# Linear attention and a feed-forward layer on one Trainium2 core: plain fp32 projections for the first two batches, and a place of its own for each loaded pair

## The chip, the cores and the metric

The kernel runs on one core of a Trainium2 chip. The metric is the device time in microseconds; the number shown is the median of three runs. Beside it stands one execution taken with the profiler, in which every instruction has a start and a length.

The engines are TensorE (matmul; the profile calls it PE, and its weight load PEld), VectorE (DVE), ScalarE (ACT), GpSimd (POOL) and SyncE (SP, which here issues all DMA transfers).

## The reference

Eight batches, eight heads, 576 tokens, head size 64; 128 features. `q`, `k` and `w_phi` are scaled so that the exponentials spread widely.

```python
def phi(x):
    proj = np.einsum('bhsd,df->bhsf', x, w_phi)
    proj = proj - np.max(np.abs(proj), axis=-1, keepdims=True)
    return np.concatenate([np.exp(proj), np.exp(-proj)], axis=-1)
q_p, k_p = phi(q), phi(k)
kv = np.einsum('bhsf,bhsd->bhfd', k_p, v)
z = np.sum(k_p, axis=2)
num = np.einsum('bhsf,bhfd->bhsd', q_p, kv)
den = np.einsum('bhsf,bhf->bhs', q_p, z)[..., None] + 1e-06
attn = (num / den).astype(np.float32)
# x: attn as 4608 tokens of 512
h = x @ w_in                       # 512 -> 2048, the weights are float64
out = np.maximum(0.01 * h, h) @ w_out   # 2048 -> 512
```

## The kernel before

**Pairs of heads.** Two heads share the 128 partitions (64 features each), so there are 32 pairs: `i = 4 * batch + pair`. Pairs 0 to 3 are batch 0 and go through `first_k_phase` and `first_q_phase`; pairs 4 to 7 are batch 1 and go through `k_phase` (its branch `nat`, for `i < NK`) and `token_q_phase`; all later pairs go through the other branch of `k_phase` and through `q_phase`, which the change leaves as they are.

**A projection.** For 128 tokens, `proj` multiplies the tokens (the stationary operand) with `bd`, a block-diagonal 128 x 256 copy of `w_phi` for both heads. It does this in three matmuls of the type float32r (`F32R`, the profile's `fp32r`): tokens and weights are both split into a high part (the value cast to float32r) and a low part (the remainder), and the products high x high (L304), high x low (L305) and low x high (L306) are summed. The splits are made once for each loaded tile: a cast for the high part (L196, L351, L452 by ScalarE, L522 by VectorE) and a subtraction for the low part (L197, L352, L453, L524). `copy_` and `tt_` (L64, L71) choose the engine: for the key's low part GpSimd and VectorE take turns, for the query's it is GpSimd. Other matmuls of these two batches, the product of exponentials and v (L212 in the branch `nat`, L484) and the numerators (L333, L567), have plain fp32 operands.

**After a projection** VectorE takes the largest absolute value of each token (L240, L317, L472, L537) and subtracts it (L243, L318, L474, L539), ScalarE makes both exponentials, TensorE the product.

**The weights.** `load_weights` brings `w_in` and `w_out` in 32 chunks as 64-bit floats through two staging places (the transfers of L154) and turns each into a high and a low float32r part: on ScalarE L159, L164 and the cast of `copy_("h")`; on VectorE L160, L161, L162, L165 and the subtraction of `tt_("l")`.

**The feed-forward part** works on 18 blocks of 256 tokens: `layer1` (L619 to L627) and `layer2` (L638 to L640), each with 16 steps over the hidden layer.

**Order.** Nothing in the text fixes the order of the instructions on an engine. A planner takes them by priority (a smaller number first) as a simulation says that their operands and places are free: first the loads of the start (`2 * PF`), then batch 0's keys and its first 256 queries (`PF`), its other queries (`PU`), the later attention (`PA`), the weights (`PW`), the feed-forward part (0). Within an engine and within SP's queue that order is then fixed, and the chip waits where an operand isn't there.

**Places.** `st(...)` takes a place from a small ring by its tag; most tags, `rk`, `rv`, `rq`, `ks` and `qs` among them, have one. A new tile with that tag waits until everything that reads the old one has run. In batch 0, pairs 0 and 2 use the places `rk` and `rv`, and pairs 1 and 3 share a place in `f2`; the loads of pairs 2 and 3 follow when the pair before them has been split or used. `fr1`, `f2`, `f3` and `fr4` are four places of 8 KB a partition which later hold the last group of weights.

## Time and profile before

| | us |
|---|---|
| median of 3 runs | 1211.63 (1211.42 to 1212.69) |
| the profiled execution | 1209.61 |
| its span, first to last instruction | 1207.8 |
| granted TensorE clock, mean | 0.992 |

| engine | busy, us | share of the span | instructions |
|---|---|---|---|
| PE | 1160.7 | 96% | 7654 |
| PEld | 1041.8 | 86% | 7654 |
| DVE | 785.4 | 65% | 1541 |
| ACT | 850.7 | 70% | 2144 |
| POOL | 437.9 | 36% | 436 |

How to read it: "busy" counts from start to end of each instruction. Matmuls overlap, so PE can look busy without doing all it could; the distance from one matmul's start to the next says more. `L304` is line 304 of the kernel; a line in a helper, such as L67 or L72, gathers all that use the helper, and the tile names (`ks<-rk`) tell them apart. In a group, `xN | busy, mean` gives count, total in us and the mean in ns, then the idle time before the group and what ended it. In a line of the timeline the columns are start, length, engine, line, operation, tiles.

### The profile page before, as it was taken

The numbers are of one execution on the slowest core, as the hardware profiler recorded it, in microseconds if no ns is written. First come the engines' busy times: TensorE is split into PE (matmuls) and PEld (weight loads), VectorE is DVE, ScalarE is ACT, GpSimd is POOL, SyncE is SP. The second block draws the span as 40 slices with busy tenths as digits, with TensorE's granted clock in tenths as the row PEclk, the third lists the DMA queues.
The fourth block names the chain that finished last, engine by engine and source line by source line (L and its number), as shares of the span: only waits on it lengthen the run. The fifth ranks groups of instructions, "written<-read, shape, count | busy, mean of one in ns | idle before, by whom it ended". The sixth has DMA issues, their size and how long they took to land.

```text
span 1207.8 us, 21459 instructions
## 1 busy us (share of the span) xinstructions
PE 1160.7 (96%) x7654; PEld 1041.8 (86%) x7654; DVE 785.4 (65%) x1541; ACT 850.7 (70%) x2144; POOL 437.9 (36%) x436
## 2 busy tenths in 40 slices
PE   6889899999998999999999999999999999999998
PEld 5578688999897988989899999998999998988987
DVE  7999864577787677677787787736777776211111
ACT  6898765778777787878888888846787877433222
POOL 3121121344544454544545454513454544210000
PEclk9999999999998999999999999999999999999999
DMA  6545421011111011111111111100111100000000
GB/s 195 149 126 150 130 80 35 22 49 31 49 32 49 21 27 43 31 49 31 49 32 49 32 40 31 49 22 28 32 49 32 49 1 19 1 18 9 10 18 18
DMA packets 62778, 57.01 MB, mean 47 GB/s; under 512 B 45136, under 2 KB 46288, under 8 KB 62672
## 3 DMA queue, kind: packets, MB, share of 16 engines
q1 hardware_dynamic: 62672, 55.65, 16.4%
q8 instruction: 60, 0.98, 0.4%
q14 instruction: 46, 0.38, 0.1%
HBM read 46.20 MB, written 9.44 MB: 46 GB/s over the span
## 4 chain that ended last, share of the span: by engine, by line
PE 76%; DVE 11%; ACT 7%; issue 3%; DMA 2%; POOL 0%; DVEq 0%; ACTq 0%
PE h L619 10%; PE h L620 10%; PE h L622 10%; PE acc L638 9%; PE acc L640 9%; PE acc L639 9%; PE c L212 6%; PE a L232 2%; PE a L422 2%; PE a L419 2%; PE a L420 2%; PE a L333 1%; DVE ql L165 1%; PE a L379 1%; PE a L380 1%
## 5 line engine op out<-in xcount | busy, mean ns | idle before, releaser
L619 PE MATMUL h<-xh,w0h 128*128 128x256 f32 x1152 | 292.3, 284 | 6.8 <-DVE gl L627 4.5
L620 PE MATMUL h<-xh,w0l 128*128 128x256 f32 x1152 | 289.7, 282 | 0.0
L627 DVE TENSOR_TENSOR gl<-h,gh 128x256 fp32r<-128x256 f32 x288 | 118.5, 416 | 237.4 <-ACT gh L67 210.9
L638 PE MATMUL acc<-w1h,gh 128*128 128x512 f32 x576 | 230.3, 400 | 6.8 <-ACT gh L67 6.1
L619 PEld LDWEIGHTS h<-xh,w0h 128*128 128x128 f32 x1152 | 217.9, 189 | 17.3 <-DVE gl L627 7.7
L639 PE MATMUL acc<-w1l,gh 128*128 128x512 f32 x576 | 228.4, 397 | 0.0
L620 PEld LDWEIGHTS h<-xh,w0l 128*128 128x128 f32 x1152 | 217.8, 189 | 6.0
L625 ACT ACTIVATE h<-h 128x256 f32<-128x256 f32 x288 | 105.3, 368 | 157.2 <-PE h L622 155.3
L640 PE MATMUL acc<-w1h,gl 128*128 128x512 f32 x576 | 204.3, 397 | 0.0
L622 PE MATMUL h<-xl,w0h 128*128 128x256 f32 x1152 | 200.1, 282 | 0.1
L72 POOL TENSOR_TENSOR ql<-eq,qh 128x576 fp32r<-128x576 f32 x96 | 146.1, 1538 | 73.0 <-ACT qh L67 47.8
L622 PEld LDWEIGHTS h<-xl,w0h 128*128 128x128 f32 x1152 | 164.3, 189 | 0.9 <-POOL xl L72 0.3
L72 POOL TENSOR_TENSOR kpl<-ek,kph 128x512 fp32r<-128x512 f32 x72 | 95.4, 1325 | 146.4 <-ACT kph L67 67.5
L638 PEld LDWEIGHTS acc<-w1h,gh 128*128 128x128 f32 x576 | 108.8, 189 | 28.4 <-ACT gh L67 9.8
L639 PEld LDWEIGHTS acc<-w1l,gh 128*128 128x128 f32 x576 | 109.0, 189 | 18.6 <-issue 0.4
L67 ACT CAST gh<-h 128x256 fp32r<-128x256 f32 x288 | 105.2, 373 | 25.6 <-PE acc L639 21.3
L72 POOL TENSOR_TENSOR xl<-ring,xh 128x256 fp32r<-128x256 f32 (+3 forms) x96 | 61.2, 669 | 155.0 <-PE h L622 135.3
L72 POOL TENSOR_TENSOR ring<-ring,mb 128x576 f32<-128x576 f32 (+2 forms) x45 | 49.8, 1108 | 175.0 <-DVE mb L342 45.5
L640 PEld LDWEIGHTS acc<-w1h,gl 128*128 128x128 f32 x576 | 99.5, 189 | 8.5 <-issue 0.4
L202 DVE TENSOR_TENSOR ks<-rk,ks 64x576 fp32r<-64x576 f32 x48 | 53.7, 1118 | 36.5 <-ACT ks L67 35.3
L250 ACT ACTIVATE ek<-pmk 128x256 f32<-128x256 f32 (+1 forms) x128 | 53.4, 417 | 24.3 <-POOL kpl L72 10.3
L212 PE MATMUL c<-kph,vh 128*66 128x256 f32 x240 | 62.3, 282 | 4.0 <-DVE kvl L295 2.2
(225 smaller groups left out, 2366.2 us busy)
## 6 DMA issues: line engine op xcount, KB each, us to landing
out_dram<-o SPq DMA_DIRECT2D x35, 256.0 KB, 2.1
rk<-in_k_dram SPq DMA_DIRECT2D x30, 288.0 KB, 2.8
ring<-in_w_in_dram SPq DMA_DIRECT2D x16, 512.0 KB, 3.6
qh<-in_w_out_dram SPq DMA_DIRECT2D x16, 512.0 KB, 3.7
rq<-in_q_dram SPq DMA_DIRECT2D x28, 288.0 KB, 3.0
rv<-in_v_dram SPq DMA_DIRECT2D x30, 256.0 KB, 3.4
rv<-in_vt_dram SPq DMA_DIRECT2D x60, 32.0 KB, 3.0
f<-in_k_dram SPq DMA_DIRECT2D x2, 288.0 KB, 4.0
```

The costliest lines, as they stand in the source:

```text
L67: nc.scalar.copy(o, i)
L72: (nc.vector if pick(key) == "v" else nc.gpsimd).tensor_tensor(o, a, b, op=op)
L202: nc.vector.tensor_tensor(ks[n, j], rk[o], ks[o, j].bitcast(F32), op=ALU.subtract)
L212: nc.tensor.matmul(kvp[0 : lt.shape[1], 256 * j : 256 * j + 256], lhsT=lt, rhs=rt, start=first and j == 0, stop=last, skip_group_check=True)
L619: nc.tensor.matmul(ph, lhsT=weight(0, "h", ft)[:, d * P : d * P + P], rhs=xh[:, d], start=d == 0, stop=False)
L620: nc.tensor.matmul(ph, lhsT=weight(0, "l", ft)[:, d * P : d * P + P], rhs=xh[:, d], start=False, stop=False)
L622: nc.tensor.matmul(ph, lhsT=weight(0, "h", ft)[:, d * P : d * P + P], rhs=xl[:, d], start=False, stop=d == NP - 1)
L625: nc.scalar.activation(ph, ph, AF.Prelu, alpha=0.01)
L627: nc.vector.tensor_tensor(gl, ph, gh.bitcast(F32), op=ALU.subtract)
L638: nc.tensor.matmul(a, lhsT=gh[:, ts], rhs=weight(1, "h", ft), start=ft == 0, stop=False)
L639: nc.tensor.matmul(a, lhsT=gh[:, ts], rhs=weight(1, "l", ft), start=False, stop=False)
L640: nc.tensor.matmul(a, lhsT=gl[:, ts], rhs=weight(1, "h", ft), start=False, stop=ft == NFT - 1)
```

## The change

`bd` becomes one plain fp32 tile, and `proj` one plain matmul that reads the loaded tile itself. The high and low parts of keys and queries of batches 0 and 1 go, with their casts and subtractions, on all of `first_k_phase`, `first_q_phase`, `k_phase` (branch `nat`) and `token_q_phase`. `rk` and `rq` are thereby read until the last projection of a phase. The four pairs of batch 0 each get a landing place for k and v (pair 0 in `rk` and `rv`; the others in `f2` and `fr1`), and all these loads are issued at the start. The second and third part of batch 0's queries land in `fr4`.

```diff
@@ -91,15 +91,13 @@
     xl = ct([P, NP, T], F32R, "xl")
     wq = ct([P, 2, F], F32R, "wq")
     wq_h, wq_l = wq[:, 0], wq[:, 1]
-    bd = st([P, 2, 2 * F], F32R, "bd")
-    bd_h, bd_l = bd[:, 0], bd[:, 1]
+    bd = ct([P, 2 * F], F32, "bd")
     vh = ct([P, 10, 66], F32R, "vh")
     vl = ct([P, 10, 64], F32R, "vl")
     nc.gpsimd.memset(vh[:, :, 64:66].bitcast(F32), 1.0)
     nc.gpsimd.memset(vl[0:64, 8:10].bitcast(F32), 0.0)
 
-    fr1, fr4 = (cp.tile([P, 2048], F32R, tag="late", name=n, bufs=4) for n in ("fr1", "fr4"))
-    f2, f3 = (cp.tile([P, 2048], F32, tag="late", name=n, bufs=4) for n in ("f2", "f3"))
+    fr1, f2, f3, fr4 = (cp.tile([P, 2048], F32, tag="late", name=n, bufs=4) for n in ("fr1", "f2", "f3", "fr4"))
 
     def part(x, i, shape):
         n = shape[0] * (shape[1] if len(shape) == 2 else 1)
@@ -109,12 +107,13 @@
     first_k, first_q = {}, {}
 
     def first_load_k(i):
-        if i % 2 == 0:
+        if i == 0:
             rk = st([P, S], F32, "rk")
             rv = st([P, 10, 66], F32, "rv")
         else:
-            rk = part(f2, 0, [S])
-            rv = part(f2, S, [10, 66])
+            x, o = (f2, 0) if i == 1 else (fr1, (i - 2) * S)
+            rk = part(x, o, [S])
+            rv = part(f2 if i % 2 else fr1, 1236 if i == 3 else S * i, [10, 66])
         nc.sync.dma_start(rk, k[i])
         first_k[i] = rk, rv
 
@@ -123,8 +122,7 @@
         nc.sync.dma_start(rv[:, 0:8, 0:64], v[i])
         nc.sync.dma_start(rv[0:64, 8:10, 0:64], vt[i])
         nc.sync.dma_start(rv[64:128, 8:10, 0:64], vt[i])
-        if i < 3:
-            nc.gpsimd.memset(rv[:, :, 64:66], 1.0)
+        nc.gpsimd.memset(rv[:, :, 64:66], 1.0)
 
     tc.cur_priority = 2 * PF
     wr = st([P, F], F32, "tq")
@@ -134,15 +132,16 @@
         first_load_k(i)
     for i in range(2):
         first_load_v(i)
+    for i in range(2, NP):
+        first_load_k(i)
+        first_load_v(i)
     nc.scalar.copy(wq_h, wr)
     nc.vector.tensor_tensor(wq_l, wr, wq_h.bitcast(F32), op=ALU.subtract)
-    nc.gpsimd.memset(bd_h.bitcast(F32), 0.0)
-    nc.gpsimd.memset(bd_l.bitcast(F32), 0.0)
+    nc.gpsimd.memset(bd, 0.0)
     for j in range(2):
         r = slice(64 * j, 64 * j + 64)
         c = slice(F * j, F * j + F)
-        nc.scalar.copy(bd_h[r, c], wr[r])
-        nc.vector.tensor_tensor(bd_l[r, c], wr[r], wq_h[r].bitcast(F32), op=ALU.subtract)
+        nc.scalar.copy(bd[r, c], wr[r])
 
     def load_weights():
         n = 0
@@ -190,12 +189,8 @@
     def k_phase(i):
         nat = i < NK
         rk, rv = kraw.pop(i)
-        ks = st([P, 2, S], F32R, "ks")
-        kh, kl = ks[:, 0], ks[:, 1]
-        if nat:
-            copy_("kh", kh, rk)
-            tt_("kl", kl, rk, kh.bitcast(F32), ALU.subtract)
-        else:
+        if not nat:
+            ks = st([P, 2, S], F32R, "ks")
             for j in range(2):
                 o, n = slice(64 * j, 64 * j + 64), slice(64 - 64 * j, 128 - 64 * j)
                 copy_("kh", ks[o, j], rk[o])
@@ -205,7 +200,8 @@
                 tt_("vl", vl[r, c], rv[r, c, 0:64], vh[r, c, 0:64].bitcast(F32), ALU.subtract)
         if i + 1 < B * NP:
             load_k(i + 1)
-        yield
+        if not nat:
+            yield
         kvp = pt("c")
 
         def kv_mm(j, lt, rt, first=False, last=False):
@@ -222,7 +218,7 @@
                 pk = pt("a")
                 for s in range(w):
                     t0 = (2 * g + s) * P if g < 2 else S - P
-                    proj(pk, s, kh[:, t0 : t0 + P], kl[:, t0 : t0 + P])
+                    proj(pk, s, rk[:, t0 : t0 + P])
                 pkv = pk[r, 0 : 256 * w].rearrange("p (a f) -> p a f", f=F)
             else:
                 for s in range(w):
@@ -299,19 +295,16 @@
     def blocks(x):
         return x.rearrange("p a b -> p (a b)").rearrange("p (c d) -> p c d", d=32)
 
-    def proj(pk, s, lh, ll, n=P):
-        o = pk[0:n, 256 * s : 256 * s + 256]
-        nc.tensor.matmul(o, lhsT=lh, rhs=bd_h, start=True, stop=False)
-        nc.tensor.matmul(o, lhsT=lh, rhs=bd_l, start=False, stop=False)
-        nc.tensor.matmul(o, lhsT=ll, rhs=bd_h, start=False, stop=True)
-
-    def q_group(qh, ql, t0, w, kvh, x, pm, dn):
+    def proj(pk, s, x, n=P):
+        nc.tensor.matmul(pk[0:n, 256 * s : 256 * s + 256], lhsT=x, rhs=bd, start=True, stop=True)
+
+    def q_group(rq, t0, w, kvh, x, pm, dn):
         pq = pt("a")
         ns = max(w // P, 1)
         n = min(w, P)
         for s in range(ns):
             c = slice(t0 + s * P, t0 + s * P + n)
-            proj(pq, s, qh[:, c], ql[:, c], n)
+            proj(pq, s, rq[:, c], n)
         m4 = st([P, 4], F32, "m4")
         pqv = pq[0:n, 0 : 256 * ns].rearrange("p (a f) -> p a f", f=F)
         nc.vector.tensor_reduce(m4[0:n, 0 : 2 * ns], pqv, axis=AX.X, op=ALU.max, apply_absolute_value=True)
@@ -346,16 +339,11 @@
     def token_q_phase(i):
         b, hp = divmod(i, NP)
         rq = qraw.pop(i)
-        qs = st([P, 2, S], F32R, "qs")
-        qh, ql = qs[:, 0], qs[:, 1]
-        copy_("qx", qh, rq)
-        tt_("qr", ql, rq, qh.bitcast(F32), ALU.subtract)
         if i + 1 < B * NP:
             load_q(i + 1)
-        yield
         tq = st([P, 2, 2, U], F32, "tq").rearrange("p a b c -> p a (b c)")
         for g, (t0, w) in enumerate(units):
-            yield from q_group(qh, ql, t0, w, kvs_of[i][0], ring[:, b % 2, hp, t0 : t0 + w],
+            yield from q_group(rq, t0, w, kvs_of[i][0], ring[:, b % 2, hp, t0 : t0 + w],
                                tq[:, g % 2, 0:DM].rearrange("p (a f) -> p a f", f=F), st([P, U], F32, "dn")[:, 0:w])
 
     def q_phase(i):
@@ -443,28 +431,15 @@
     def first_k_phase(i):
         od = i % 2
         rk, rv = first_k.pop(i)
-        if od:
-            kh = part(fr1, 0, [S])
-            kl = part(fr1, S, [S])
-        else:
-            ks = st([P, 2, S], F32R, "ks")
-            kh, kl = ks[:, 0], ks[:, 1]
-        copy_("kh", kh, rk)
-        tt_("kl", kl, rk, kh.bitcast(F32), ALU.subtract)
-        if i + 2 < NP:
-            first_load_k(i + 2)
-            if not od:
-                first_load_v(i + 2)
-        elif i + 2 == NP:
+        if i + 2 == NP:
             load_k(NP)
-        yield
         kvp = pt("h")
         for g in range(3):
             pk = pt("a" if od else "acc")
             w = 2 if g < 2 else 1
             for s in range(w):
                 t0 = (2 * g + s) * P if g < 2 else S - P
-                proj(pk, s, kh[:, t0 : t0 + P], kl[:, t0 : t0 + P])
+                proj(pk, s, rk[:, t0 : t0 + P])
             r = slice(0, P) if g < 2 else slice(64, P)
             n = P if g < 2 else 64
             m4 = st([P, 4], F32, "m4")
@@ -496,8 +471,6 @@
         nc.scalar.copy(kvh[:, :, :, 0:64], kvtv[:, :, :, 0:64])
         nc.scalar.copy(kvh[:, :, :, 64:P], kvtv[:, :, :, 64:65].broadcast_to([P, 2, 2, 64]))
         kvs_of[i] = kvh, None
-        if i == 1:
-            first_load_v(3)
         yield
 
     r0 = ring[:, 0].rearrange("p a s -> p (a s)")
@@ -508,30 +481,26 @@
     def first_load_q(u):
         t0, w = units[u]
         if u == 0:
-            rq, qh, ql = st([P, NP, w], F32, "qs"), xh, part(fr4, 0, [NP, w])
+            rq = st([P, NP, w], F32, "qs")
         elif u == 1:
-            rq, qh, ql = part(f3, 1024, [NP, w]), part(fr4, 1024, [NP, w]), part(fr4, 0, [NP, w])
+            rq = part(fr4, 0, [NP, w])
         else:
-            rq, qh, ql = st([P, NP, w], F32, "rq"), part(fr1, 1152, [NP, w]), part(fr1, 1408, [NP, w])
+            rq = part(fr4, 1024, [NP, w])
         nc.sync.dma_start(rq, q[0:NP, :, t0 : t0 + w].rearrange("a p t -> p a t"))
-        first_q[u] = rq, qh, ql
+        first_q[u] = rq
 
     def first_q_phase(u):
         t0, w = units[u]
-        rq, qh, ql = first_q[u]
-        nc.vector.tensor_copy(qh, rq)
-        for hp in range(0, NP, 2):
-            tt_("ql", ql[:, hp : hp + 2], rq[:, hp : hp + 2], qh[:, hp : hp + 2].bitcast(F32), ALU.subtract)
-        yield
+        rq = first_q[u]
         tail = u == 2
         if tail:
-            qh, ql = (x.rearrange("p a t -> p (a t)").unsqueeze(1) for x in (qh, ql))
+            rq = rq.rearrange("p a t -> p (a t)").unsqueeze(1)
             w = NP * w
         n, ns = P, 2
         for hp in range(1 if tail else NP):
             pq = pt("a" if u else "acc")
             for s in range(ns):
-                proj(pq, s, qh[:, hp, s * P : s * P + n], ql[:, hp, s * P : s * P + n], n)
+                proj(pq, s, rq[:, hp, s * P : s * P + n], n)
             m4 = st([P, 4], F32, "m4")
             pqv = pq[0:n, 0 : 256 * ns].rearrange("p (a f) -> p a f", f=F)
             nc.vector.tensor_reduce(m4[0:n, 0 : 2 * ns], pqv, axis=AX.X, op=ALU.max, apply_absolute_value=True)
```

## The prediction

> **What bounds the kernel now.** I read the page first, then stretches of the span, then the groups of VectorE in the stretch that the change touches.
>
> ```profile
> span 1207.8 us, 21459 instructions
> PE 1160.7 (96%) x7654; PEld 1041.8 (86%) x7654; DVE 785.4 (65%) x1541; ACT 850.7 (70%) x2144; POOL 437.9 (36%) x436
> ```
>
> The page says TensorE, 96%, and VectorE two thirds. Both are averages over stages, and the change touches only the first of them. So I asked for the two stretches around the first block of the feed-forward part (each row: stretch, length, busy time and count of PE, PEld, DVE, ACT, POOL, then clock and DMA):
>
> ```profile
> 6.40:167.00 160.60, 141.06 (x811) 112.98 (x811) 149.64 (x288) 130.96 (x293) 31.43 (x34) 0.96 0.50 142
> 167.00:246.00 79.00, 78.93 (x512) 69.13 (x512) 39.98 (x82) 49.14 (x137) 20.49 (x30) 1.00 0.15 40
> ```
>
> Until 167 us VectorE works 149.64 of 160.6 us, and TensorE does 811 instructions, 5.0 per us; behind it TensorE does 6.5 per us and VectorE half as much. 167 us is no arbitrary place:
>
> ```profile
> L165 DVE CUSTOM_DVE_ANT_0 ql<-ql,kvl x32: 641/682/1619, 23.2 to 165.1; 128x1024 uint16<-128x1024 uint16 x32
> ```
> ```profile
> 166.95 0.28 PE L619 MATMUL h<-xh,w0h 128*128 128x256 f32 x1
> ```
>
> The last of the 32 weight chunks goes through L165 at 165.1, and layer 1 of block 1 begins at 166.95. So: up to about 166 us the kernel is paced by VectorE, which prepares the weights and does the reductions of batches 0 and 1; afterwards by TensorE. The change has two currencies. VectorE time saved before 166 us moves the start of block 1; TensorE time added behind it is paid in full.
>
> **TensorE: one projection of 128 tokens.** Old: three reduced-precision matmuls. New: one plain one, which the trace shows as two instructions (kv products and L333 are of this kind already). Pieces of the chain, start and time until the next:
>
> ```profile
> 160.05 0.12 PE a L304
> 160.17 0.12 PE a L305
> 160.29 0.12 PE a L306
> ...
> 162.16 0.86 PE a L333 x4
> ```
>
> Old: three pieces at 0.118 (160.05 to 160.29 is two), 0.355 us a projection. New: 0.86 / 4 = 0.215 per instruction, 0.43 a projection, with the same 128 columns of weights. So +0.075 us each. [...] How many lie where:
>
> ```profile
> 0.00:167.00 167.00, 21.88 (x62) 13.43 (x62) 0.96 0.50 142
> 167.00:246.00 79.00, 5.60 (x16) 2.87 (x16) 1.00 0.15 40
> ```
>
> (L304 alone, first matmul of each projection.) 78 in all: 62 before 167 us, where TensorE has gaps (62 x 0.075 = 4.7 us against 19.5 us not busy, so I cost them at nothing as long as VectorE paces), and 16 behind it: 16 x 0.075 = **+1.2 us**. If the cover is gone, all 78 count: +5.9 us.
>
> **VectorE: what goes.** In 0 to 167 us, the removed groups:
>
> ```profile
> L72 DVE TENSOR_TENSOR fr<-f,fr 128x576 fp32r<-128x576 f32 x2 | 3.3, 1674 | 0.8 <-ACT fr L67 0.8
> ...
> L72 DVE TENSOR_TENSOR ks<-rk,ks 128x576 fp32r<-128x576 f32 x1 | 0.8, 759 | 0.2 <-ACT ks L67 0.2
> ...
> L522 DVE CAST fr<-f 128x1024 fp32r<-128x1024 f32 x1 | 0.7, 685 | 0.0
> L522 DVE CAST xh<-qs 128x1024 fp32r<-128x1024 f32 x1 | 0.7, 684 | 0.0
> L522 DVE CAST fr<-rq 128x256 fp32r<-128x256 f32 x1 | 0.6, 578 | 0.0
> ```
>
> Together **-6.1 us**. The two subtractions of L145 lie at 5 us, ahead of the stretch, and count for nothing.
>
> **GpSimd beside VectorE.** The same 576-wide subtraction takes 0.76 us in one group above and 1.67 in the other; I take it that the slow ones share something with GpSimd. The weight operations spread likewise:
>
> ```profile
> L165 DVE CUSTOM_DVE_ANT_0 ql<-ql,kvl 128x1024 uint16<-128x1024 uint16 x32 | 23.6, 738 | 0.4
> L160 DVE TENSOR_SCALAR ql<-ql 128x512 f32<-128x512 f32 x32 | 14.7, 459 | 2.8 <-ACT ql L159 2.6
> L161 DVE TENSOR_SCALAR ql<-ql 128x512 int32<-128x512 int32 x32 | 14.2, 444 | 0.2
> L72 DVE TENSOR_TENSOR w1l<-ql,w1h 128x512 fp32r<-128x512 f32 x16 | 12.2, 762 | 0.5 <-ACT w1h L67 0.4
> L162 DVE SCALAR_TENSOR_TENSOR ql<-qh,ql 128x512 int32<-128x512 int32 x16 | 12.1, 756 | 0.1
> ```
> ```profile
> 162.62 0.68 DVE L72 TENSOR_TENSOR w0l<-ql,w0h 128x512 fp32r<-128x512 f32 x1
> 163.22 0.42 DVE L161 TENSOR_SCALAR ql<-ql 128x512 int32<-128x512 int32 x1
> ```
>
> Against 0.68 and 0.42 for single ones, the means hold 32 x 0.056 + 32 x 0.04 + 32 x 0.024 + 16 x 0.08 + 16 x 0.075, about 6.3 us too much. Of GpSimd's 31.4 us in the stretch the change removes:
>
> ```profile
> L72 POOL TENSOR_TENSOR ks<-rk,ks 128x576 fp32r<-128x576 f32 x4 | 5.9, 1481 | 16.6 <-ACT ks L67 16.6
> ...
> L72 POOL TENSOR_TENSOR fr<-f,fr 128x512 fp32r<-128x512 f32 x2 | 3.3, 1656 | 4.5 <-DVE fr L522 4.5
> L72 POOL TENSOR_TENSOR fr<-qs,xh 128x512 fp32r<-128x512 f32 x2 | 3.1, 1573 | 0.0
> L72 POOL TENSOR_TENSOR qs<-rq,qs 128x576 fp32r<-128x576 f32 x2 | 3.0, 1524 | 7.8 <-ACT qs L67 7.8
> ```
>
> 15.3 us, half. Estimate: half of 6.3, **-3.2 us** (ends 0 and -6.3; I take the middle, in proportion to the time). ScalarE loses nine casts of 0.67, 6 us of 131; it is not the bound, so nothing. The bd, wq and memset edits are ahead of the stretch: nothing.
>
> **The start.**
>
> ```profile
> 9.36 0.69 DVE L472 TENSOR_REDUCE m<-acc 128x4 f32<-128x512 f32 x1 [1.40 <-PE acc L306]
> ```
> ```profile
> 10.43 0.49 SPq L154 DMA_DIRECT2D ring<-in_w_in_dram  x1
> ```
> ```profile
> 16.25 0.67 ACT L159 ACTIVATE ql<-ring 128x512 f32<-128x512 f32 x1
> ```
> ```profile
> 30.56 0.67 PE L484 MATMUL h<-ring,rv 128*66 128x256 f32 x1 [2.23 <-DMA rv<-in_v_dram]
> ```
>
> The first reduction waited 1.40 us for the matmul on the low part; that idle time goes, **-1.4 us**, and the first reduction should come near 7 us. The kv product of pair 2 waited until 30.56 for v, whose place was occupied; now the loads of pairs 2 and 3 are issued ahead, and the key phases of batch 0 should end some 8 us sooner. That is no gain by itself, since VectorE did weights in the meantime. Against it: six more transfers stand on SP's queue ahead of the first weights at 10.43; at 0.49 us of issue or a little more each, some 3 to 3.6 us. The first weights land at about 20 us instead of 16.25. Until then VectorE can only reduce what TensorE gives it: a key phase is 15 plain projections and products, 15 x 0.43 = 6.5 us of TensorE, for two and a half pairs of a reduction and a subtraction of 0.69 each, 3.5 us of VectorE. From 7 to 20 us that leaves it idle for 13 - 13 x 3.5 / 6.5 = 6.0 us. I take **+5.5 us** (ends: 2, if some weights come earlier; 8, if the clock of TensorE is still low at the start and the weights are pushed back further).
>
> **Waits added.** rk and rq have one place each, and now the next load waits for the last projection instead of the last split. Before: cast 0.67 and subtraction 1.48 stood between; now a transfer.
>
> ```profile
> rk<-in_k_dram SPq DMA_DIRECT2D x30, 288.0 KB, 2.8
> ```
> ```profile
> 136.88 0.37 PE L304 MATMUL a<-bd,ks 128*128 128x256 f32 x1
> ```
> ```profile
> 147.87 0.56 PE L304 MATMUL a<-bd,ks 128*128 128x256 f32 x1
> ```
>
> That is some 1 us more, seven times. The last projection of one key phase (136.88) and the first of the next (147.87) are 11 us apart, so it is covered: nothing, and up to +7 if the cover were gone. Queued behind such a load on SP are the v loads, which wait for the end of the phase anyway, and weight transfers, which would wait with it; they have two stages, and a stall costs at most one chunk's pace once (160.6 / 32 = 5.0 us). In the first query unit the tile of the loaded q is also the place of pair 1's exponentials, which so wait for the projections of pair 3: at most two projections, 0.9 us, with weight work on VectorE meanwhile, nothing.
>
> **Sum.** Start of block 1: -6.1 - 3.2 - 1.4 + 5.5 = -5.2 us. Behind it +1.2. Together -4.0. The profiled execution took 1209.61 us (span 1207.8), so 1205.6 in its terms; the median of the runs is 1211.63, 2.0 above it: **1207.6**.
>
> **Rivals.** About 0.2%, 2.4 us, is what a measurement of this kernel can tell from no change: 1209.2 to 1214.1 is "the same".
>
> *No change (0.25).* The idle time at the start is at its upper end, 8 us, and the GpSimd relief is near 1 instead of 3.2: -6.1 - 1 - 1.4 + 8 + 1.2 = +0.7, 1212.3. For it: the weights are two thirds of VectorE's work before 167 us, and nothing in the change feeds them earlier. Against it: the reductions of pairs 2 and 3 can fill the gap now that their loads come first.
>
> *Slower (0.20).* TensorE, not VectorE, sets the start of block 1, and all 78 projections are on the path: +5.9, 1217.5. It decides as soon as block 1 starts less than 1.2 us earlier. For it: 141.06 of 160.6 us is 88% busy already. Against it: those 811 instructions overlap, and their rate is three quarters of the later one.
>
> *Larger gain (0.15).* VectorE isn't idle at the start (the 2 us end): -6.1 - 3.2 - 1.4 + 2 + 1.2 = -7.5, 1204.1; with the full 6.3 us from GpSimd 1201.0.
>
> *Forecast (0.40):* 1205 to 1210, own range, most of it under 1209.2.
>
> **How the numbers follow.** Faster: the larger gain, and nearly all of the forecast's share (0.38), with a little of the no-change case at its lower edge, 0.55. Same: 0.24. Slower: 0.21. The range that leaves out 2 in 10 takes in the larger gain to 1201 and the slower case up to 1216.
>
> **What the profile would show.** The first reduction near 7 us and the first weight cast near 20 us, with VectorE idle in between; the kv products without the gap before 30.56; the weight operations nearer to 0.68 and 0.42 in the mean; 0.43 us for each projection; layer 1 of block 1 at about 162 us, and every later block earlier by 4. It is wrong if block 1 moves by less than 1.2 us, if the weight transfers stand behind a blocked rk load on SP's queue, or if the order of the instructions, which is planned anew, makes the blocks after 246 us longer: the work there is the same, so any difference would come from the order alone.

## The result and the profile after

| | before | after |
|---|---|---|
| median of 4 runs, us | 1211.53 (1210.53 to 1212.69) | 1202.33 (1198.88 to 1203.50) |
| ratio | 1 | 0.9919, 95% interval 0.9896 to 0.9942 |
| profiled execution / its span, us | 1209.61 / 1207.8 | 1203.5 / 1201.7 |
| block 0, block 1 begin, us | 64.6, 166.9 | 57.5, 170.0 |
| block 4, block 5 begin, us | 370.5, 445.2 | 369.8, 445.8 |
| block 5 to the end, us | 762.5 | 755.8 |
| TensorE: work / idle, us | 1121.8 / 86.0 | 1127.9 / 73.8 |

The gain is 9.2 us in the medians and 6.1 in the two profiled executions; the profiled run of the changed kernel is the slowest of its four. Of the executions of the experiments below, one of e5 took 2308.87 us, nearly twice the others, and is left out of e5's median. "Work" is the sum of TensorE's instructions at their undisturbed start-to-start prices in the traces (0.118 us for 256 reduced-precision columns, 0.215 for a plain fp32 instruction, and so on), and "idle" is the span less the work. Both are estimates: a price that is 1% off moves every total by 11 us the same way, so the differences between kernels say more than the totals. "Idle" also holds what TensorE loses in stretches where its granted clock is 0.50: the traces have 20.5 us of such stretches before and 17.1 after. In the one of before at 387 us, reduced-precision matmuls of 256 columns start 0.21 us apart instead of 0.12, so by estimate such stretches cost up to half their length. A block begins with its first matmul of layer 1 (every 64th; line L619 before, L588 to L591 after). The old lines have moved: projections L304 to L306 are L299, the weights L159 to L165 are L158 to L164, the weight DMA L154 is L153.

The head of the page of the changed kernel, and the two stretches that the prediction read (columns as there):

```profile
span 1201.7 us, 21253 instructions
PE 1166.0 (97%) x7576; PEld 1042.1 (87%) x7576; DVE 771.0 (64%) x1532; ACT 847.1 (70%) x2132; POOL 417.8 (35%) x422
...
6.40:167.00 160.60, 146.32 (x744) 112.49 (x744) 141.20 (x282) 127.44 (x282) 14.14 (x20) 0.97 0.49 141
167.00:246.00 79.00, 79.00 (x493) 68.10 (x492) 39.69 (x83) 48.99 (x137) 18.34 (x28) 1.00 0.17 46
```

To 167 us VectorE has 141.20 us of work instead of 149.64, and GpSimd 14.14 instead of 31.43. So the relief is there. But it turned into idle time (11.0 before, 19.4 now), and block 1 did not come earlier:

```profile
169.96 0.39 PE L588 MATMUL h<-xh,w0h 128*128 128x256 f32 x1
```

Where VectorE idles is seen at the start (start, duration, engine, line, operation; in brackets the idle time before it and what ended it):

```profile
7.66 0.69 DVE L447 TENSOR_REDUCE m<-acc 128x4 f32<-128x512 f32 x1 [2.75 <-PE acc L299]
...
15.44 0.43 SPq L153 DMA_DIRECT2D ring<-in_w_in_dram  x1
...
22.79 0.65 ACT L158 ACTIVATE ql<-ring 128x512 f32<-128x512 f32 x1
23.48 0.43 DVE L159 TENSOR_SCALAR ql<-ql 128x512 f32<-128x512 f32 x1 [5.36 <-ACT ql L158]
```

The first weights are issued at 15.44 (10.43 before) and cast at 22.79 (16.25). Directly before, TensorE is full while VectorE has three instructions in 6 us:

```profile
18.00:24.00 6.00, 6.00 (x28) 3.77 (x27) 0.64 (x3) 2.98 (x7) 0.12 (x1) 1.00 0.77 270
```

Over the whole stretch the waits of VectorE for weights (wait, us in total, times, longest) were `ql L160 <- ACT ql L159: 2.6, 5, 0.7` before and are now

```profile
DVE ql L159 <- ACT ql L158: 9.5, 7, 5.4
DVE m L447 <- PE acc L299: 2.7, 1, 2.7
```

The queue of SP takes part in that behind the start too. Up to 168 us SP stood 13.7 us for the places of v loads (6.8 before) and 9.2 for those of k loads (6.4 before). A stretch of the chain (start, time until the next piece, what) has weights behind v loads (L176, L177) that stood for the end of a key phase:

```profile
83.28 5.11 DMA qh<-in_w_out_dram
...
115.25 0.57 SPq L176
115.88 0.65 SPq L177
116.59 0.59 SPq L178
117.28 4.35 DMA qh<-in_w_out_dram
```

Then the gain must come from behind. From the start of block 5 to the start of block 8 (before, then after), TensorE takes 6.1 us less, though not one of the instructions there was edited. About 0.8 us of that is work which the new order puts ahead of block 5; the rest is idle time:

```profile
445.20:642.50 197.30, 192.06 (x1319) 175.76 (x1318) 151.07 (x285) 157.25 (x400) 100.45 (x91) 1.00 0.14 37
```
```profile
445.80:637.00 191.20, 190.57 (x1314) 175.01 (x1312) 142.57 (x282) 157.76 (x400) 96.51 (x89) 1.00 0.14 38
```

The waits that the profile lists for TensorE there add up to 5.0 us before and 0.5 after. The three that the timeline shows best (in brackets the idle time) are nowhere in after:

```profile
518.16 0.33 PE L212 MATMUL c<-kph,vh 128*66 128x256 f32 x1 [0.73 <-ACT kph L67]
526.57 0.51 PE L638 MATMUL acc<-w1h,gh 128*128 128x512 f32 x1 [0.76 <-ACT gh L67]
584.21 0.39 PE L619 MATMUL h<-xh,w0h 128*128 128x256 f32 x1 [1.45 <-DVE gl L627]
```

So three questions were open: where VectorE's relief went, why block 5 begins at the same time whatever block 1 does, and whether the 6.7 us behind block 5 are order alone. TensorE's order of instructions differs from before up to block 10 and is the same from block 11 on.

### The profile page after: what moved, and what is told of

It reads as the page before. It is cut to its first block, busy times and chain, and to the rows that moved or that the text cites. A ratio compares the mean times of both kernels' runs of the same rounds, so it can differ in the third digit from the quotient of the medians.

```text
span 1201.7 us, 21253 instructions
## 1 busy us (share of the span) xinstructions
PE 1166.0 (97%) x7576; PEld 1042.1 (87%) x7576; DVE 771.0 (64%) x1532; ACT 847.1 (70%) x2132; POOL 417.8 (35%) x422
## 3 DMA queue, kind: packets, MB, share of 16 engines
q1 hardware_dynamic: 62672, 55.65, 16.4%
## 4 chain that ended last, share of the span: by engine, by line
PE 84%; ACT 6%; DVE 5%; DMA 2%; issue 1%; SPq 0%; POOL 0%; DVEq 0%; ACTq 0%
PE h L588 11%; PE h L589 11%; PE h L591 11%; PE acc L607 10%; PE acc L608 10%; PE acc L609 10%; PE c L208 7%; PE a L228 2%; PE a L408 2%; PE a L410 2%; PE a L407 2%; PE a L299 1%; DMA qh<-in_w_out_dram 1%; PE a L326 1%; PE a L367 1%
## 5 line engine op out<-in xcount | busy, mean ns | idle before, releaser
L588 PE MATMUL h<-xh,w0h 128*128 128x256 f32 x1152 | 294.6, 285 | 3.2 <-DVE gl L596 1.4
L588 PEld LDWEIGHTS h<-xh,w0h 128*128 128x128 f32 x1152 | 218.4, 190 | 14.6 <-DVE gl L596 3.4
L591 PE MATMUL h<-xl,w0h 128*128 128x256 f32 x1152 | 198.0, 282 | 0.0
L72 POOL TENSOR_TENSOR ql<-eq,qh 128x576 fp32r<-128x576 f32 x96 | 144.5, 1520 | 75.3 <-ACT qh L67 61.1
L591 PEld LDWEIGHTS h<-xl,w0h 128*128 128x128 f32 x1152 | 163.8, 189 | 0.5
L72 POOL TENSOR_TENSOR kpl<-ek,kph 128x512 fp32r<-128x512 f32 x72 | 95.4, 1325 | 154.2 <-ACT kph L67 65.3
L72 POOL TENSOR_TENSOR ring<-ring,mb 128x576 f32<-128x576 f32 (+2 forms) x45 | 50.8, 1129 | 213.3 <-DVE mb L546 58.5
L72 POOL TENSOR_TENSOR xl<-ring,xh 128x256 fp32r<-128x256 f32 (+3 forms) x96 | 60.2, 657 | 150.7 <-PE h L591 110.3
L246 ACT ACTIVATE ek<-pmk 128x256 f32<-128x256 f32 (+1 forms) x128 | 53.3, 417 | 25.8 <-POOL kpl L72 10.7
```

The lines of the kernel that those rows point to most:

```text
L72: (nc.vector if pick(key) == "v" else nc.gpsimd).tensor_tensor(o, a, b, op=op)
L588: nc.tensor.matmul(ph, lhsT=weight(0, "h", ft)[:, d * P : d * P + P], rhs=xh[:, d], start=d == 0, stop=False)
L591: nc.tensor.matmul(ph, lhsT=weight(0, "h", ft)[:, d * P : d * P + P], rhs=xl[:, d], start=False, stop=d == NP - 1)
```

## The experiments

All times are medians; ratios are against the kernel before on the same chip (1211.59, 1211.62 and 1211.81 us in the three groups e1 to e4, e5 to e8 and e9 to e11). The table gives TensorE's idle time by place, in the profiled execution of each, which can lie some 3 us from its kernel's median.

| kernel | median us, ratio [95%] | block 1 / 4 / 5 begins | block 5 to end | idle before block 0 / in 0 / 1 to 3 / 4 / 5 to 8 / rest |
|---|---|---|---|---|
| before | 1211.53 | 166.9 / 370.5 / 445.2 | 762.5 | 25.3 / 18.7 / 7.9 / 10.0 / 9.1 / 15.0 |
| after | 1202.33, 0.9919 [0.9896, 0.9942] | 170.0 / 369.8 / 445.8 | 755.8 | 15.5 / 23.6 / 6.8 / 9.7 / 3.9 / 14.4 |
| e1 | 1205.67, 0.9952 [0.9935, 0.9969] | 160.9 / 363.5 / 448.8 | 756.0 | 19.3 / 16.4 / 7.7 / 15.1 / 4.4 / 13.9 |
| e2 | 1201.36, 0.9923 [0.9897, 0.9948] | 156.8 / 361.4 / 443.8 | 755.9 | 15.7 / 15.8 / 8.4 / 13.6 / 3.9 / 14.5 |
| e3 | 1220.77, 1.0079 [1.0051, 1.0108] | 153.8 / 369.5 / 453.6 | 764.8 | 17.1 / 17.3 / 14.4 / 14.3 / 9.7 / 17.7 |
| e4 | 1208.35, 0.9977 [0.9962, 0.9992] | 167.7 / 370.3 / 446.9 | 762.7 | 26.8 / 20.4 / 6.2 / 9.7 / 9.5 / 15.3 |
| e5 | 1206.32, 0.9954 [0.9938, 0.9971] | 168.2 / 368.1 / 442.7 | 760.8 | 15.5 / 21.8 / 6.8 / 9.1 / 8.3 / 14.2 |
| e6 | 1207.92, 0.9971 [0.9957, 0.9984] | 167.7 / 370.5 / 443.4 | 759.9 | 25.9 / 18.8 / 7.2 / 8.1 / 7.8 / 13.7 |
| e7 | 1231.19, 1.0159 [1.0138, 1.0180] | 158.4 / 377.2 / 471.5 | 760.2 | 18.7 / 9.2 / 13.6 / 23.6 / 6.6 / 15.8 |
| e8 | 1201.20, 0.9920 [0.9900, 0.9939] | 166.1 / 366.5 / 435.2 | 763.2 | 14.7 / 20.6 / 5.5 / 4.3 / 8.1 / 17.5 |
| e9 | 1198.59, 0.9893 [0.9880, 0.9907] | 167.4 / 369.5 / 441.0 | 755.8 | 15.5 / 21.0 / 7.9 / 6.2 / 3.8 / 14.4 |
| e10 | 1205.63, 0.9943 [0.9930, 0.9957] | 160.3 / 365.9 / 443.4 | 760.5 | 17.6 / 17.4 / 7.7 / 10.7 / 8.3 / 14.3 |
| e11 | 1201.49, 0.9918 [0.9905, 0.9932] | 169.0 / 368.8 / 445.1 | 755.4 | 15.1 / 23.0 / 6.7 / 10.0 / 3.9 / 13.9 |

**e1: the landing places undone, the plain projections kept.**

```
-        if i == 0:
+        if i % 2 == 0:
...
-            x, o = (f2, 0) if i == 1 else (fr1, (i - 2) * S)
-            rk = part(x, o, [S])
-            rv = part(f2 if i % 2 else fr1, 1236 if i == 3 else S * i, [10, 66])
+            rk = part(f2, 0, [S])
+            rv = part(f2, S, [10, 66])
...
+            if g == 2 and i + 2 < NP:
+                first_load_k(i + 2)
+                if not od:
+                    first_load_v(i + 2)
```

> The change with its plain projections, but loads and places of batch 0 as before (pairs 2 and 3 land where pairs 0 and 1 were, after their last projection). Theory 'start' (the early loads close TensorE's gap before block 0, 25.3 us of idle time down to 15.5, and that is the gain): block 0 begins at 62 to 65 us again and the time is 1208 to 1212. Theory 'splits' (the casts and subtractions that went are the gain): it stays at 1201 to 1204. Theory 'order' (the gain lies in blocks 1 to 8, where TensorE's idle time fell by 7 us because the planner's order came out otherwise): the total is anywhere from 1199 to 1210 and follows the idle time in blocks 1 to 8, not the start of block 1.

The first weight cast went back to 14.71 us and block 1 to

```profile
160.94 0.47 PE L591 MATMUL h<-xh,w0h 128*128 128x256 f32 x1
```

That is 6.0 us ahead of before with the casts and subtractions gone and the old landing places, and 9.1 ahead of after. The relief is real; the late weights take it. Yet block 5 begins at 448.8, later than in both, since block 4 idles 15.1 us instead of 10. Of the three theories, "start" missed (block 0 begins at 61.3, the time is below its range) and "splits" missed; the time lies in the wide range of "order", though the idle time in blocks 1 to 8, 27.2 us, is that of before (27.0).

**e2: as after, but the first two weight chunks are issued ahead of the loads of pairs 2 and 3.**

```
+    for raw, src in zip(stages, (w_in, w_out)):
+        nc.sync.dma_start(raw, src[:, 0].bitcast(I32))
...
-                nc.sync.dma_start(raw, src[:, ft].bitcast(I32))
+                if ft:
+                    nc.sync.dma_start(raw, src[:, ft].bitcast(I32))
```

> The changed kernel, with the transfers of the first two weight chunks issued ahead of the loads of pairs 2 and 3. If the late weights cost what the prediction said (VectorE idle at the start, first cast of weights at 22.8 instead of 16.25 us) and VectorE paces up to block 1: first cast near 15 us, block 1 at 163 to 166 instead of 170.0, total 1196 to 1199. If the pace up to block 1 is set by something else (the two staging places and their transfers, or TensorE): block 1 stays within 2 us of 170 and the total at 1200 to 1204.

The first cast came at 11.7 us, block 1 at 156.81, ten earlier than before, and block 4 at 361.4, nine earlier. Block 5:

```profile
156.81 0.47 PE L591 MATMUL h<-xh,w0h 128*128 128x256 f32 x1
...
443.77 0.28 PE L591 MATMUL h<-xh,w0h 128*128 128x256 f32 x1
```

1.5 us of ten arrive there; block 4's idle grew to 13.6. The time, 1201.36, can't be told from after's, and is not the 1196 to 1199 that was expected of an earlier block 1. So the start of block 1, on which the prediction's sum rests, was worth next to nothing in this kernel.

**What block 4 waits for.** Its tokens 1152 to 1279 are in batch 2, in pairs 8 to 11, and the last multiplication of pair 11 stands on GpSimd at the same time in before and in after. Directly behind it comes the cast of block 4's last tokens, which waited for it:

```profile
376.69 1.56 POOL L72 TENSOR_TENSOR ring<-ring,mb 128x576 f32<-128x576 f32 x1 [2.01 <-DVE mb L431]
...
378.28 0.30 ACT L67 CAST xh<-ring 128x128 fp32r<-128x128 f32 x1 [1.49 <-POOL ring L72]
```
```profile
376.86 1.56 POOL L72 TENSOR_TENSOR ring<-ring,mb 128x576 f32<-128x576 f32 x1 [1.88 <-DVE mb L419]
...
378.45 0.30 ACT L67 CAST xh<-ring 128x128 fp32r<-128x128 f32 x1 [1.36 <-POOL ring L72]
```

In e2 the multiplication stands at 375.64, in e1 at 385.03.

**e8: the gate by itself.** For pairs 8 to 11 the kernel leaves out the subtractions that make the low parts; the matmuls on them read the high parts instead.

```
-                    tt_("kpl", kpl, ek, kph.bitcast(F32), ALU.subtract)
+                    if i < 12: kpl = kph
+                    else: tt_("kpl", kpl, ek, kph.bitcast(F32), ALU.subtract)
...
-                tt_("ql", ql, eq, qh.bitcast(F32), ALU.subtract)
+                if i < 12: ql = qh
+                else: tt_("ql", ql, eq, qh.bitcast(F32), ALU.subtract)
```

> The changed kernel without the subtractions for the low parts of the exponentials in pairs 8 to 11: the matmuls on them read the high parts instead, so TensorE's work is the same and GpSimd and VectorE lose about 28 instructions of 1.1 to 1.6 us in the chain of these pairs. If block 4's start is held by the attention of pairs 8 to 11 (idle time of 9.7 us there), block 4's wait falls to 2 to 5 us and the total by 4 to 8: 1194 to 1198. If the time is set by TensorE's work alone and the wait is bound to appear elsewhere: 1200 to 1204.

Block 4 (stretch, length, busy times, clock, DMA), after, then e8:

```profile
369.80:445.80 76.00, 70.90 (x469) 64.78 (x468) 57.93 (x109) 59.57 (x151) 38.48 (x39) 0.96 0.13 36
```
```profile
366.50:435.20 68.70, 66.97 (x450) 61.52 (x449) 52.19 (x102) 54.12 (x138) 35.30 (x34) 0.98 0.13 36
```

Block 5 begins 10.6 us earlier than in after, at 435.2, and block 4 idles 4.3 instead of 9.7, as expected. That the pairs' chain holds block 4 is shown. In the five kernels that share after's order up to block 0 (after, e5, e8, e9, e11), block 5 begins 67.4 to 69.3 us behind the multiplication of pair 11, wherever that stands between 367.18 and 376.86; with other orders the distance is another (62.0 in e6, 63.8 in e1). The total of e8 nevertheless is 1201.20 and missed its 1194 to 1198: the plan gave blocks 5 to 10 an order of its own, and from block 5 to the end it took 763.2 instead of 755.8.

**e9: the same gate eased in a complete kernel.** Of the 28 such subtractions on GpSimd, 12 go to VectorE (the lines are broken here to fit).

```
-                    tt_("kpl", kpl, ek, kph.bitcast(F32), ALU.subtract)
+                    (nc.vector if i < 12 and c % 2 or c == 3 else nc.gpsimd).tensor_tensor(
+                        kpl, ek, kph.bitcast(F32), op=ALU.subtract)
...
-                tt_("ql", ql, eq, qh.bitcast(F32), ALU.subtract)
+                (nc.vector if i < 12 and u else nc.gpsimd).tensor_tensor(
+                    ql, eq, qh.bitcast(F32), op=ALU.subtract)
```

> The changed kernel, complete, with half of the low-part subtractions of pairs 8 to 11 (of the query's exponentials, and some of the key's) moved from GpSimd, where they take 1.3 to 1.5 us, to VectorE. TensorE's order is that of the changed kernel up to block 1 and again from block 6 on. If block 4 waits for the chain of pairs 8 to 11: its idle time falls from 9.7 to 4 to 7 us, block 5 begins 3 to 6 us before 445.8, and as the order behind it is unchanged the total falls by as much, to 1197 to 1200. If it doesn't wait for that chain: 1201 to 1204.

```profile
373.52 1.57 POOL L72 TENSOR_TENSOR ring<-ring,mb 128x576 f32<-128x576 f32 x1 [1.56 <-DVE mb L419]
...
369.50:441.00 71.50, 68.16 (x460) 62.42 (x459) 58.71 (x106) 56.85 (x143) 35.55 (x32) 0.98 0.13 34
```

Pair 11 is done 3.3 us earlier, block 4 idles 6.2 instead of 9.7 (1.7 of that is a shorter stretch at half clock, 3.4 us instead of 6.8), and block 5 begins 4.8 earlier, at 441.0. Its order from block 6 on is that of after, and so is the time behind (755.8). Here a gain at the gate did arrive, in the size expected: 1198.59, the fastest of all, 3.7 below after and 2.9 below e11, which ran beside it; its range (1198.06 to 1198.76) lies below both of theirs.

**e10: e9 and e2 together.**

> The same, with the first two weight chunks issued ahead of the loads of pairs 2 and 3 as well; TensorE's order from block 6 on is that of the kernel before. Theory: block 1 near 157 us, block 5 earlier than 443.8, and 4 to 5 us given back in blocks 6 to 8 by that order: 1200 to 1204. If the order behind is worth nothing: 1195 to 1199.

1205.63, above what was expected. Two reasons are in its trace: block 4 waits 10.7 us (the planned order places the pairs' chain otherwise, and the ease is gone), and its order from block 6 on is exactly before's, with before's stalls: 760.5 behind block 5. Two good edits gave a worse plan.

**e11: the changed kernel once more**, beside e9 and e10.

> The changed kernel once more, beside the two above: 1200 to 1204, block 5 at 444 to 447 us.

1201.49, and the same places of its idle time. So neither the gain over before nor the lead of e9 comes from the chip or the day.

**e5: the changed kernel with the order of before behind.** A copy of two columns in pair 5, some 0.16 us of VectorE by estimate (the reciprocal of the same size, L341 in before, takes 0.16 at 156.89). What it writes is read by nothing; it is there to make the planner choose otherwise.

```
+    nudge = ct([P, 2], F32, "nudge")
...
+    i == 5 and g == 1 and nc.vector.tensor_copy(nudge, m4[:, 0:2])
```

> The changed kernel with one more VectorE instruction, a copy of two columns in pair 5 (some 0.1 us). It leaves TensorE's order in blocks 1 to 3 almost as it is, and from block 6 on gives exactly the order of the kernel before. Theory 'order': TensorE's idle time in blocks 5 to 8 rises from 3.9 us to that of the kernel before, about 8 to 9, with the same stalls of 0.9 to 1.6 us, and the total is 1205 to 1208. Rival (the gain is the change's own, from the work that went): 1201 to 1204.

TensorE's order from block 6 on came out exactly as before's, and the three stalls are back, at the same matmuls:

```profile
514.48 0.33 PE L208 MATMUL c<-kph,vh 128*66 128x256 f32 x1 [0.73 <-ACT kph L67]
522.88 0.50 PE L607 MATMUL acc<-w1h,gh 128*128 128x512 f32 x1 [0.72 <-ACT gh L67]
580.57 0.39 PE L588 MATMUL h<-xh,w0h 128*128 128x256 f32 x1 [1.37 <-DVE gl L596]
...
442.70:639.00 196.30, 192.10 (x1320) 176.25 (x1319) 149.89 (x284) 157.21 (x400) 99.40 (x91) 1.00 0.14 37
```

196.30 us for a stretch that took before 197.30 and after 191.20. 1206.32 in all: 4.0 above after, 5.3 below before, in the range of "order". So some 4 to 5 us of the gain of 9.2 are an order behind block 5 that the change hit upon. The whole table bears this out. The four kernels with before's order from block 6 on (before, e4, e5, e10) take 760.5 to 762.7 us from block 5 to the end, the four with after's (after, e2, e9, e11) 755.4 to 755.9, and e3 and e8, which share a third order, 764.8 and 763.2, whatever came ahead of them.

**e4 and e6: the kernel before with the same copy**, in pair 5 and in pair 6 (`i == 6 and g == 1`).

> The kernel before with one more VectorE instruction, a copy of two columns in pair 5 (some 0.1 us of work), which lets the planner put some 390 instructions of TensorE in another order from there on. Theory 'order': the total moves by more than its own work, 2 to 8 us either way, in blocks 1 to 10. Rival (the order is worth nothing, and the changed kernel's gain has another cause): 1210.5 to 1212.5, as before.

> The kernel before with the same small copy in pair 6: the order up to block 0 is that of the kernel before, and from block 8 on that of the changed kernel; blocks 1 to 7 are in an order of their own. Theory 'order': idle time in blocks 5 to 8 falls from 9.1 to 4 to 5 us, the total is 1204 to 1208 although all casts and subtractions are still there. Rival: 1210 to 1213.

e4 missed its aim: the order from block 6 on stayed that of before, and so did the time behind (762.7). Its median is 3.2 lower, of which its trace shows nothing (block 5 begins 1.7 later than in before), but that trace is of the slowest of its ten executions, 1211.40 us at a mean granted clock of 0.992; the fastest took 1205.90 at 0.996. The mean is 0.9932 over the ten and 0.9915 over the sixteen of before beside them, and that difference is 2.1 us of 1210. So most of the 3.2 goes along with the granted clock; why the clock was higher is open. e6 got after's order from block 8 on, with an own one in blocks 1 to 7; behind block 5 it takes 759.9 (before 762.5), in all 1207.92, 3.7 less than before without anything of the change in it, at a mean clock no higher than that of before beside it (0.9906 against 0.9912). Its idle time in blocks 5 to 8 fell to 7.8, not to the 4 to 5 expected.

**e7: is the added work of TensorE hidden?** Each of the 38 projections of the first phases is made twice.

```
-                proj(pk, s, rk[:, t0 : t0 + P])
+                proj(pk, s, rk[:, t0 : t0 + P]); proj(pk, s, rk[:, t0 : t0 + P])
...
-                proj(pq, s, rq[:, hp, s * P : s * P + n], n)
+                proj(pq, s, rq[:, hp, s * P : s * P + n], n); proj(pq, s, rq[:, hp, s * P : s * P + n], n)
```

> The changed kernel with every projection of batch 0 issued twice (38 more of 0.43 us, 16.4 us of TensorE, all before about 75 us). If, as predicted, TensorE's gaps up to block 1 hide such work: block 1 moves by 0 to 5 us and the total by 0 to 4 (1202 to 1206). If every projection is paid wherever it lies: 1217 to 1220. If block 4's wait for the attention of batch 2 sets the time, the total moves by what the chain of the pairs is delayed, 5 to 12: 1207 to 1214.

38 x 0.43 = 16.3 us more work, and 28.9 us more time than after: not hidden, more than the work, and above all three ranges. Block 1 begins as early as 158.40, so up to there the added work is hidden; but block 4 idles 23.6 us and block 5 begins at

```profile
471.49 0.28 PE L588 MATMUL h<-xh,w0h 128*128 128x256 f32 x1
```

Some of the excess may be the clock, which was half in this execution twice for 13.7 us between 387 and 418 (mean 0.82 from 369.8 to 445.8); but another one, at a mean clock of 0.993, still took 1228.78. The waits listed in block 4 are for operands of the attention, the longest 3.2 us for the high parts of keys' exponentials (`kph`) and 1.6 for those of queries (`qh`). They belong to pairs behind 11: the multiplication of pair 11 stands at 374.46, ahead of block 4. So what comes late is again the attention, but e7 doesn't show the gate of pair 11.

**e3: more of the same relief.** The addition that joins the weights' low bits is left out, 23 us of VectorE.

```
-    nc.vector.tensor_tensor(wi, wi, cr, op=ALU.add)
```

> The changed kernel without the addition of the weights' low bits (32 VectorE instructions of 0.68 to 0.74 us, about 23 us; the weights lose their last bits). If VectorE paces the stage up to block 1, block 1 begins 15 to 23 us earlier than 170.0 and the total falls by 12 to 20 us. If the chain transfer, ScalarE, VectorE, release of the staging place paces it, block 1 moves by 0 to 5 us, since this instruction stands behind the release. If TensorE paces it: 0 to 2 us.

```profile
153.81 0.47 PE L588 MATMUL h<-xh,w0h 128*128 128x256 f32 x1
...
453.57 0.36 PE L588 MATMUL h<-xh,w0h 128*128 128x256 f32 x1
```

Block 1 begins 16.2 us earlier and the kernel is 18.4 us slower than after. For the first half the prediction's reading holds: VectorE paces block 1. The second half is the opposite of what every theory expected of the total: the pairs of batch 2 run later (the transposes of pair 8's kv stand at 264 us, 250 in after), block 5 begins 7.8 later, and the time behind is 764.8. Why the plan puts the attention back when the feed-forward can start sooner isn't settled; that a sooner block 1 takes TensorE from the pairs is the simplest reading, but no run shows it alone. The time behind block 5 goes with the order, which is that of e8 from block 6 on.

## Why the prediction was right or wrong, point by point

The direction was right and the time lies in the range, near its lower end; the gain of 9.2 is more than twice the forecast's 4.0, and the time is outside the forecast's own 1205 to 1210. The reason given is not the reason found, so that the time fell inside the wide range is in good part luck. It lies where the rival "Larger gain" stood (1204.1 to 1201.0), but that rival's condition, a VectorE that isn't idle at the start, did not hold: it idles more than before.

- **0.43 us a projection, +5.9 us for all 78: held.** TensorE's work grew by 6.1 us, and the chain of the changed kernel shows a projection as

```profile
163.03 0.43 PE a L299 x2
```
- **"VectorE paces block 1", with -6.1, -3.2, -1.4: held in size.** The first reduction came 1.7 us earlier, at 7.66 ("near 7"), though its own wait grew from 1.40 to 2.75; VectorE's work to 167 us fell by 8.4 (9.3 forecast, 6.1 for the operations and 3.2 for the GpSimd relief), and the mean excess of the weight operations over 0.68 and 0.42 fell from 6.3 to about 3.6 us:

```profile
L164 DVE CUSTOM_DVE_ANT_0 ql<-ql,kvl 128x1024 uint16<-128x1024 uint16 x32 | 23.3, 727 | 1.5 <-ACT kvl L163 1.0
...
L72 DVE TENSOR_TENSOR w1l<-ql,w1h 128x512 fp32r<-128x512 f32 x15 | 10.4, 694 | 1.9 <-ACT w1h L67 1.8
```

  Two thirds of that are in the subtractions of L72 (762 to 694 ns) and one form of the joining at L161 (756 to 710); L164 hardly moved (738 to 727). That GpSimd goes with the slow ones shows in before: up to 167 us, the 8 weight subtractions of L72 that run beside a GpSimd instruction take 0.86 us in the mean, the other 24 take 0.68. The kv products of pair 2 no longer wait for v; they begin at 25.87 instead of 30.56.
- **"+5.5 for the weights later": mis-sized.** The start of block 1 was to move by -5.2 and moved by +3.1, so the term is some 8 us too small. The first cast came 6.5 us later (3 to 3.6 forecast), and weights stood behind blocked loads on SP's queue, the case that the prediction named as one that would make it wrong. e1 and e2, which bring the weights back, have block 1 at 160.9 and 156.8, the 162 of the prediction and better. The upper end, 8, named a low clock at the start: before's reduced-precision matmuls start 0.21 us apart from 6.34 to 9.97 us and 0.12 from 10.16 on, and the first 8 plain instructions of after take 3.55 us, 0.44 each, all at a granted clock of 1.00. What this does to the weights no run shows.
- **"Waits added: nothing": not tried alone.** SP's waits for the places of k loads rose from 6.4 to 9.2 us up to 168 us, those of q loads fell from 5.9 to 4.4. How much of the late block 1 that is, no run shows.
- **"and every later block earlier by 4": the step that failed.** A block's start was taken to hand its gain to the next. Block 4 instead waits for the attention of pairs 8 to 11, whose last multiplication begins at 376.7 and 376.9 us. Against before, e1 and e2 lose 10.6 and 7.6 us between the starts of block 4 and block 5, partly to idle time and partly because more of the attention's work stands in block 4. e8 and e9 shift block 5 by easing that chain.
- **"62 projections cost nothing, TensorE has gaps": held for the start of block 1, failed for the total.** In e7 block 1 begins early with 16.3 us more work ahead of it, and e3 shows that VectorE paces it; so the slower rival, in which TensorE sets the start of block 1, is not what happened, although its sign (block 1 less than 1.2 us earlier) was there. But e7 pays for all of what is added there and more. In the profiled executions TensorE has until block 5 some 6.9 us more work (0.8 of it moved ahead by the order) and 6.3 us less idle time (-9.8 before block 0, +4.9 in it, -1.4 in blocks 1 to 4), and block 5 begins 0.6 us later. Six of the 9.8 come without the early loads, since e1 idles 19.3 us there. So a gain in idle time and the dearer projections cancel up to block 5; that one ate the other is the reading of this sum, and no run shows it alone.
- **"behind it +1.2": -6.7 behind block 5.** The prediction's last sentence named order alone as the thing that could change the time there and counted only a loss. It was a gain, and e5 returns 4 to 5 of it with the edited work in place. With before's order behind, the change is worth 5.3 us (ratio 0.9954, 0.9938 to 0.9971). That this is near the forecast's 4.0 is not a confirmation: e5's block 5 begins 2.5 us ahead of before's and after's own 0.6 behind, and e4 and e6 move by 3.2 and 3.7 with nothing of the change in them.

What stays open: how the 5.3 splits into the change, the plan of blocks 1 to 5 and the granted clock; and what makes the plan of e3 put the attention back. The clock may be a large part: its mean over the executions is 0.9945 in after, 0.994 in e5 and 0.9913 in the 35 of before, and 0.003 of 1210 is 3.6 us. Whether the change brings fewer stretches at half clock, or the plan does, wasn't tried.

## What to carry to other kernels

Before a stage's gain is carried to the end of the kernel, look in the trace of before for the next place where TensorE idles and ask what ends that wait: here the chain of pairs 8 to 11, which stood at 377 us before and after although the stage ahead was tuned. Split the span into work at undisturbed prices and idle time by place; it shows at once that work rose by 6.1 and idle time fell by 12.2, and where. Where the order of the instructions is planned anew with every edit, compare at the same order, or nudge the plan with an operation that costs next to nothing, before a few us are credited to the edit. And set the granted clock of the executions beside their times: the four of after go from 1198.88 us at 0.997 to 1203.50 at 0.993.

## What was not expected

- A copy of some 0.16 us that nobody reads goes with -3.2, -3.7 and +4.0 us in the total (e4, e6, e5). Each is more than the 0.2% that a measurement here can tell from nothing, and none of it is work. For e5 the order behind is shown as the cause; most of e4's goes with the granted clock.
- 23 us less work on the engine that paces the first 170 us made the kernel 18.4 us slower (e3).
- The granted clock falls to 0.50 in single stretches of 3.4 or 6.8 us, three times in the profiled execution of before (27.2, 146.6 and 385.6 us) and four times in that of after (64.4, 119.0, 149.7 and 385.2). The one at 385 stands right behind block 4's waits in both, where TensorE has little to do; before, in 3.4 us each (clock in the third column from the right):

```profile
383.40:386.80 3.40, 0.78 (x3) 0.30 (x2) 3.34 (x7) 1.34 (x3) 1.04 (x3) 0.82 0.42 122
386.80:390.20 3.40, 3.33 (x16) 3.36 (x17) 3.16 (x11) 1.89 (x5) 0.45 (x1) 0.50 0.58 143
```

The matmuls behind the wait run at half the clock, 16 in 3.4 us: from 387.12 to 389.26 they start 0.21 us apart, from 379.03 to 379.62 it was 0.12. In the 3.4 us ahead of the stretch TensorE was busy for 1.47 us before and 1.26 after. If the waits bring the low clock, they cost more than their idle time; that they do was not tried here by itself.
